# Widening the first inverses of a delta-rule kernel two steps at a time, with 64-row operands

## The chip, the cores and the metric

The kernel runs on one core of a Trainium2 chip. The metric is the device time of one execution in microseconds; the time before is a median of three runs.

## The reference

A linear attention with a delta rule (4 batches, 8 heads, 768 positions, head size 48) is followed by a gated MLP over the 384 joined channels. All is float32.

```python
k_n = k / (norm(k) + 1e-06)
for t in range(S):
    y[t]  = q[t] @ state
    v_old = k_n[t] @ state
    state = state + beta[t] * outer(k_n[t], v[t] - v_old)
x = y joined over heads                               # (4, 768, 384)
h = relu(x @ w_in); u, v = halves of h                # 1024 -> 512 + 512
v_n = (v - mean(v)) / sqrt(var(v) + 1e-06)
v_s = w_spatial @ v_n + b_spatial[:, None]            # over the 768 positions
out = (u * v_s) @ w_out
```

## The kernel before

**Tiling.** The positions are cut into chunks of 64, 12 per batch pair; two batch pairs give 24 steps (`NP`), each with 16 batch-head pairs laid out as 8 blocks (`NS`) on 128 partitions (two halves of 64). Within a chunk the recurrence is solved with the inverse of a unit triangular 64x64 matrix per batch and head. These inverses don't depend on the state, so they are made ahead of the steps, for groups of four steps (`GP`), six groups in all.

**Inverses.** `prep(g)` multiplies the keys with themselves on TensorE (`kk`), copies the products to SBUF, transposes the 32x32 diagonal blocks on VectorE so that one block lies along a partition (L651), scales them (L672), and solves them lane by lane (`lanes`, or `lanes16` for group 0) on the engine that `LANES` names: VectorE for groups 0, 2, 4, 5, GpSimd for groups 1 and 3. A second transposition (L730) puts the result back. Group 0 (`G16 = 1`) is solved for 16x16 blocks only, to have it sooner. `widen16(s)` then joins two 16x16 inverses to one 32x32, and `widen(g)` joins two 32x32 to one 64x64 for each step of the group, in five stages (`stage(f, e)`), where stage k finishes step k-1 and begins step k.

**`widen16` before.** For one step: a VectorE transposition of the blocks into `tn6` (L796); a TensorE burst E of 32 calls (8 blocks, 4 strips of 32 rows), each a 32x16 stationary block `kd` against a 32x16 one (L798); ScalarE negates the result into `gi` (L812); a burst F of 32 calls with 16-row operands (L805); VectorE adds the result into the block (L814); two half copies (L427) and two clears (L819) move the odd blocks to their place. `kd` is a copy of 16-column blocks made once (L654). Each float32 call is two matmul instructions in the trace, so a burst is 64 of them. All instructions of TensorE carry L587, the line of `mm`; the operand names tell them apart, and `kd` and `tn6` are parts of the tile `bbc`.

**Steps.** `step(s)` has five TensorE bursts (`a_`, `qs`, `b_`, `c_`, `pu`), with copies on ScalarE (L901, L931) and updates on VectorE (L872, L914, L916) between them; `b_` is the first that uses the 64x64 inverse. Two steps give one column block `J` of x, on which `mlp(J)` runs the first product of the MLP; `norm_v` makes mean and variance: ScalarE sums (L974, L984), and small instructions on VectorE (L981, L986, `fin`) work on two columns. After steps 11 and 23 `gate(b)` runs the spatial product and the output.

**What sets the order.** Every operation is added to a plan with an engine (or several to choose from), a cost in us, its reads and writes, and a priority: a due time (`due(s) = 38 + 8 s`) plus a correction from the table `TUNE`, one number per kind of operation. `Plan.run` is a list scheduler that simulates the engines with these costs and emits the instructions in the order of their planned starts. So each engine's order is fixed when the kernel is built, and every engine works its queue in order. `adv` and `execute` model TensorE's clock and its supply of instructions; `warm` fills idle TensorE time with products of `fl` that nobody reads. DMAs are all issued on SP.

**Storage.** Early tiles lie in storage that later holds weights and others. `kd` and `tn6` lie where the bias is loaded later; the raw parts of w_out and w_sp are loaded through two halves of `g0` (the pool `st`).

Of the kernel before, what the change touches and what calls it, by code (L numbers as in the profile page):

```python
# [1214 lines left out]
```

## Time and profile before

| | before |
|---|---|
| median of 3 runs | 471.94 us (469.5 to 472.24) |
| profiled execution | 473.46 us, its span 471.8 us |
| mean granted TensorE clock | 0.928 |
| busy: TensorE, VectorE, ScalarE, GpSimd | 424.1, 286.7, 239.4, 162.6 us |
| DMA | 40.67 MB |

The span runs from the first to the last instruction; all times within the trace count from its start. PE is TensorE, PEld its weight loads, DVE VectorE, ACT ScalarE, POOL GpSimd, SP SyncE. A granted clock of 1.00 is 2.4 GHz, 0.50 is 1.2 GHz.

### The profile page before, as it was taken

Reading aid. Unit: us, or ns where it says so; the run is one execution under the profiler, and the core shown is the slowest. Engines: PE = TensorE matmul, PEld = TensorE weight load, DVE = VectorE, ACT = ScalarE, POOL = GpSimd, SP = SyncE. Lnnn points to the kernel's source line nnn. Section 1 sums busy time; section 2 is a strip of 40 time slices with the busy share of each in tenths; the row PEclk is TensorE's granted clock in tenths of the full one; section 3 lists DMA queues with packets and bytes.
Section 4 is the critical chain, followed back from the end, with each engine's and each line's share of the span. In section 5 each row is a group of like instructions: output and inputs, shape, how many; then the busy total and the mean of one; then the engine's idle time right before and its main releaser. Section 6 shows DMA issues by size and latency. Waiting matters only on the chain.

```text
span 471.8 us, 20342 instructions
## 1 busy us (share of the span) xinstructions
PE 424.1 (90%) x9080; PEld 378.3 (80%) x9080; DVE 286.7 (61%) x635; ACT 239.4 (51%) x519; POOL 162.6 (34%) x294
## 2 busy tenths in 40 slices
PE   5827767998878999898999999999999999999997
PEld 4625666786766778787789999988899999999996
DVE  3998999998899964543399975423235222452340
ACT  3978737587941646994321248355323861131122
POOL 3339699883786985012217220000000000000000
PEclk9787555799978999999999999999999999999999
DMA  7950322651433452334433300133000011000002
GB/s 275 370 150 2 83 60 73 190 154 41 115 85 95 139 157 64 107 106 137 138 95 118 92 18 20 42 94 97 8 11 0 2 63 40 1 35 33 35 18 84
DMA packets 24456, 40.67 MB, mean 86 GB/s; under 512 B 3792, under 2 KB 14160, under 8 KB 24368
## 3 DMA queue, kind: packets, MB, share of 16 engines
q1 hardware_dynamic: 24368, 39.37, 27.2%
q8 instruction: 71, 1.16, 1.1%
q14 instruction: 17, 0.14, 0.1%
HBM read 33.46 MB, written 4.72 MB: 81 GB/s over the span
## 4 chain that ended last, share of the span: by engine, by line
PE 61%; DVE 15%; ACT 12%; DMA 5%; issue 4%; POOL 3%; SPq 1%; ACTq 0%; POOLq 0%; DVEq 0%
PE ps L587 61%; DMA bn<-in_bun 3%; DVE ps L697 2%; DVE prod L692 2%; ACT gt L984 1%; ACT vr L998 1%; ACT xt L788 1%; ACT vf L1006 1%; ACT pi L784 1%; ACT xt L427 1%; DVE pt L846 1%; DMA wout_h<-in_k_t 1%; DMA xs<-xs 1%; DVE ut L503 1%; DVE wla L482 1%
## 5 line engine op out<-in xcount | busy, mean ns | idle before, releaser
L587 PE MATMUL ps<-wsp_h,vf 128*128 128x256 f32 x480 | 96.6, 284 | 0.0
L587 PEld LDWEIGHTS ps<-wsp_h,vf 128*128 128x128 f32 x480 | 77.8, 188 | 0.9
L484 POOL TENSOR_TENSOR bn<-bn,nn 128x384 f32<-128x384 f32 x24 | 22.1, 920 | 95.7 <-DMA bn<-in_bun 41.2
L1065 DVE TENSOR_TENSOR gt<-ps,bbc 128x512 f32<-128x512 f32 x24 | 16.6, 690 | 53.6 <-PE ps L587 53.5
L692 POOL TENSOR_TENSOR wsp_h<-wsp_h 128x31 f32<-128x31 f32 (+15 forms) x62 | 36.8, 594 | 8.2 <-DVE wsp_h L672 6.1
L587 PE MATMUL ps<-wlb,vf 128*128 128x256 f32 x140 | 39.4, 281 | 0.0
L697 POOL TENSOR_TENSOR wsp_h<-wsp_h 128x60 f32<-128x60 f32 (+15 forms) x60 | 36.5, 609 | 1.7
L587 PE MATMUL ps<-bn 64*64 64x64 f32 x832 | 21.0, 244 | 14.2 <-DVE pt L846 6.3
L587 PEld LDWEIGHTS ps<-bn 64*64 64x64 f32 x832 | 17.3, 153 | 18.9 <-DVE pt L846 7.3
L697 DVE TENSOR_TENSOR ps<-ps,prod 128x192 f32<-128x192 f32 (+13 forms) x90 | 29.5, 328 | 2.3
L692 DVE TENSOR_TENSOR prod<-ps,la 128x192 f32<-128x192 f32 (+13 forms) x90 | 28.7, 319 | 2.2
L1070 ACT CAST xt<-gt 128x512 fp32r<-128x512 f32 x12 | 7.4, 620 | 41.9 <-DVE gt L482 41.8
L587 PE MATMUL ps<-wla,vf 128*128 128x256 f32 x100 | 28.1, 281 | 0.0
L1086 ACT COPY ob<-ps 128x384 f32<-128x384 f32 x24 | 11.5, 480 | 30.6 <-PE ps L587 24.8
L587 PE MATMUL ps<-wout_h,g 128*128 128x384 f32 x96 | 26.4, 342 | 0.0
L587 PEld LDWEIGHTS ps<-wlb,vf 128*128 128x128 f32 x140 | 26.3, 188 | 0.0
L587 PE MATMUL ps<-wout_h,xt 128*128 128x384 f32 x96 | 25.6, 338 | 0.0
L587 PE MATMUL ps<-wsp_h,bn 128*128 128x256 f32 x96 | 23.3, 281 | 0.0
L1030 ACT ACTIVATE ut<-ps 128x256 f32<-128x256 f32 x48 | 15.6, 377 | 13.8 <-PE ps L587 13.7
L1070 ACT CAST g<-gt 128x512 fp32r<-128x512 f32 x12 | 7.4, 619 | 28.5 <-DVE gt L482 21.1
L901 ACT COPY w<-ps 128x384 f32<-128x384 f32 x24 | 11.5, 479 | 19.9 <-PE ps L587 19.7
L846 DVE TENSOR_TENSOR pt<-ps,fl 128x512 f32<-128x512 f32 x24 | 16.3, 680 | 6.7 <-PE ps L587 6.6
(255 smaller groups left out, 1190.2 us busy)
## 6 DMA issues: line engine op xcount, KB each, us to landing
bn<-in_bun SPq DMA_DIRECT2D x44, 224.0 KB, 3.1
bn<-in_bun SPq DMA_DIRECT2D x48, 192.0 KB, 3.2
out<-ob SPq DMA_DIRECT2D x24, 192.0 KB, 1.9
vf<-in_w_in SPq DMA_DIRECT2D x6, 512.0 KB, 8.3
ke<-in_k_t SPq DMA_DIRECT2D x12, 224.0 KB, 3.0
g<-in_w_sp SPq DMA_DIRECT2D x6, 384.0 KB, 3.5
g<-in_w_out SPq DMA_DIRECT2D x4, 384.0 KB, 5.7
xs<-xs SPq DMA_DIRECT2D x22, 48.0 KB, 2.7
```

The source lines that it names most:

```text
L427: (nc.scalar.copy if e == "ACT" else ENG[e].tensor_copy)(out=out_, in_=in_)
L482: nc.vector.scalar_tensor_tensor(out=out, in0=in0, scalar=1.0, in1=in1, op0=ALU.mult, op1=op)
L484: nc.gpsimd.tensor_tensor(out=out, in0=in0, in1=in1, op=op)
L587: nc.tensor.matmul(o, l, r, start=start, stop=stop)
L692: P.add(eng, cost(n * m), lambda: ENG[eng].tensor_tensor(out=dst if fst else pt, in0=w[:, :n, j : j + 1].broadcast_to([128, n, m]), in1=la ...
L697: P.add(eng, cost(n * m), lambda: ENG[eng].tensor_tensor(out=dst, in0=dst, in1=pt, op=ALU.add), rd=[pk], wr=[key], pr=p0 + 2)
L846: P.add("DVE", 0.69, lambda: nc.vector.tensor_tensor(out=pt.rearrange("p (d c t) -> p d c t", d=2, t=64), in0=pq.rearrange("p (d c) -> p d ...
L901: P.add("ACT", 0.48, lambda: nc.scalar.copy(out=v3(w, 192), in_=v3(pc, 512)[:, :, 0:192]), rd=["pc"], wr=[("w", s % 2)], pr=pr)
L1030: nc.scalar.activation(out=dst[:, :, o * 128 : o * 128 + 128], in_=src[:, :, j], func=AF.Relu)
L1065: P.add("DVE", 0.69, lambda: nc.vector.tensor_tensor(out=gt(), in0=v3(bank(h.unit), 256), in1=bbc[0][:, th * 256 : th * 256 + 256].unsquee ...
L1070: P.add("ACT", 0.6, lambda: nc.scalar.copy(out=gv(gg)[0][:, hs], in_=gt_[t.unit]), rd=[kk], wr=[("gh", b, th, half)], pr=q)
L1086: P.add("ACT", 0.48, lambda: nc.scalar.copy(out=ob_[t.unit], in_=bank(h.unit)[:, :DM]), rd=[("po", b, th, o)], wr=[("ob", b, th, o)], pr=d ...
```

## The change

- `widen16(s)` works on two steps: it is called for s = 0 and 2. Both bursts use 64-row operands, 16 blocks by 2 halves, 32 calls each.
- The 64-row operands hold zeros outside their blocks. For E this is `e16` (2048 columns, cleared at the start, in the storage of group 4's inverses), for F `f16_()` (1024 columns in `g0`). They are filled by `masked`: a copy over all 128 partitions with a scale per partition, 1 in every second strip of 32 partitions and 0 in the others (`cst[:, 5:7]`), on ScalarE or GpSimd, two copies per operand.
- `kd` goes. The two halves of `g0` enter the pool `st` only after the last F.
- The clears after `widen` of the later groups may also go to ScalarE.
- In `norm_v` L981 and L986 go from VectorE to ScalarE.
- Some planner costs change, and all of `TUNE`; with it the order of every engine.

```diff
-    cst = new("cst", 4)
+    cst = new("cst", 7)
-    kd, tn6 = aux[:, 0:512], aux[:, 512:768]
+    tn6 = aux[:, 0:512]
+    e16 = tagged("xt1", GP * NS * 64)
+    def f16_():
+        return g0_()[:, 0:1024]
-    gi = early[4][:, 2048:2176]
+    gi = early[4][:, 2048:2304]
+    def masked(e, out_, in_, k):
+        if e == "ACT":
+            nc.scalar.activation(out=out_, in_=in_, func=AF.Copy, scale=cst[:, 5 + k : 6 + k])
+        else:
+            nc.gpsimd.tensor_scalar(out=out_, in0=in_, scalar1=cst[:, 5 + k : 6 + k], scalar2=None, op0=ALU.mult)
...
+    P.add("POOL", 0.5, lambda: nc.gpsimd.memset(e16, 0.0), wr=["E"], pr=-8)
-    P.pool("st", [0, 1])
+    P.pool("st", [])
...
         if g < G16:
-            P.add("ACT", 0.6, lambda: nc.scalar.copy(out=v3(kd, 16), in_=xg()[:, :, 0:16]), ...)
+            for k in range(2):
+                P.add("", {"ACT": 0.62, "POOL": 1.1}, lambda e, k=k: masked(e, v3(e16, 64)[:, :, k * 32 : k * 32 + 16], xg()[:, :, 0:16], k), ...)
...
     def widen16(s):
-        P.add("DVE", 0.44, lambda: nc.vector.transpose(out=v3(tn6, 32), in_=x8_()[:, :, 0:32]), rd=zd, wr=["tn6"], pr=pr)
+        P.add("DVE", 0.68, lambda: nc.vector.transpose(out=v3(tn6, 32), in_=x8_()[:, :, 0:32]), rd=zd, wr=["tn6"], pr=pr)
+        for k in range(2):
+            P.add("", {"ACT": 0.62, "POOL": 1.1}, lambda e, k=k: masked(e, v3(f16_(), 64)[:, :, k * 32 : k * 32 + 32], v3(tn6, 32), k), rd=["tn6", "cst"], wr=[F[k]], pr=pr)
         def e():
-            for q in range(NS):
-                for k in range(4):
-                    r = slice(32 * k, 32 * k + 32)
-                    mm(bank(u.unit)[32 * k : 32 * k + 16, q * 16 : q * 16 + 16], kd[r, (b0 + q) * 16 : (b0 + q) * 16 + 16], x8[r, q, 16:32])
+            for q in range(2 * NS):
+                for a in range(2):
+                    r = slice(64 * a, 64 * a + 64)
+                    mm(bank(u.unit)[r, q * 16 : q * 16 + 16], e16[r, (b0 + q) * 64 : (b0 + q) * 64 + 64], x8[r, q, 16:32])
         def f():
-            for q in range(NS):
-                for k in range(4):
-                    h = slice(32 * k, 32 * k + 16)
-                    mm(bank(u.unit)[32 * k : 32 * k + 32, 256 + q * 16 : 256 + q * 16 + 16], tn6[h, q * 32 : q * 32 + 32], gi[h, q * 16 : q * 16 + 16])
+            for q in range(2 * NS):
+                for a in range(2):
+                    r = slice(64 * a, 64 * a + 64)
+                    mm(bank(u.unit)[r, 256 + q * 16 : 256 + q * 16 + 16], f16_()[r, q * 64 : q * 64 + 64], gi[r, q * 16 : q * 16 + 16])
-        P.add("PE", 0.55, e, mode=3, ...)
+        P.add("PE", 1.86, e, mode=1, ...)
-        P.add("PE", 0.6, f, mode=4, ...)
+        P.add("PE", 1.86, f, mode=1, ...)
+        if s == G16 * GP - 2:
+            P.add("X", 0.0, None, wr=F, give=[("st", i) for i in range(2)])
...
     def norm_v(J, i0, i1):
-        P.add("DVE", 0.19, lambda: nc.vector.tensor_scalar_mul(out=f(1), in0=f(0), scalar1=-1.0 / DH), ...)
+        P.add("ACT", 0.2, lambda: nc.scalar.mul(out=f(1), in_=f(0), mul=-1.0 / DH), ...)
-        P.add("DVE", 0.19, lambda: nc.vector.tensor_scalar(out=f(3), in0=f(2), scalar1=1.0 / DH, scalar2=EPS, op0=ALU.mult, op1=ALU.add), ...)
+        P.add("ACT", 0.2, lambda: nc.scalar.activation(out=f(3), in_=f(2), func=AF.Identity, scale=1.0 / DH, bias=cst[:, 3:4]), ...)
...
-            for k in range(GP if g < G16 else 0):
+            for k in range(0, GP if g < G16 else 0, 2):
                 widen16(s + k)
```

Left out of the diff: the new table `TUNE`; the planner's costs of a DMA's landing (1.2 to 1.6), of the MLP's chunks (0.232, 0.117, 0.175 per matmul to 0.236, 0.119, 0.178), of a clear of 1056 columns (1.0 to 0.5) and of GpSimd's half copies (1.05 to 0.9).

## Rows read from the trace of the kernel before

**Rows 1.** The page's first part: busy us, share of the span, instructions.
```profile
PE 424.1 (90%) x9080; PEld 378.3 (80%) x9080; DVE 286.7 (61%) x635; ACT 239.4 (51%) x519; POOL 162.6 (34%) x294
```

**Rows 2.** Windows by stage: length, busy us (x instructions), granted clock, DMA share, GB/s.
```profile
43.90:77.92 34.02, 22.13 (x1097) 19.60 (x1089) 30.46 (x73) 21.25 (x45) 28.38 (x52) 0.57 0.24 64
...
83.60:118.30 34.70, 33.43 (x944) 26.44 (x945) 30.52 (x65) 24.77 (x53) 24.37 (x44) 0.92 0.44 126
118.30:163.20 44.90, 38.12 (x1237) 31.74 (x1237) 41.01 (x105) 23.80 (x61) 36.57 (x76) 0.89 0.38 109
163.20:244.40 81.20, 75.17 (x2232) 63.43 (x2232) 43.58 (x90) 49.93 (x114) 26.83 (x40) 1.00 0.40 115
244.40:471.80 227.40, 223.39 (x2932) 212.30 (x2932) 99.42 (x214) 84.11 (x187) 19.73 (x41) 1.00 0.14 44
```

**Rows 3.** The chain that ended last: start us, us, what.
```profile
45.05 1.79 issue
...
83.58 10.94 PE ps L587 x298
```

**Rows 4.** Timeline: start us, us, engine, line, operation, operands, shape, count.
```profile
40.14 2.25 DVE L730 STREAM_TRANSPOSE wla<-wl 128x1024 f32<-128x1024 f32 x1
...
47.04 0.69 PE L587 MATMUL ps<-ke 64*64 64x64 f32 x32
...
52.21 1.13 PE L587 MATMUL ps<-ke 64*64 64x64 f32 x32
...
78.80 1.05 PE L587 MATMUL ps<-bn,wla 64*64 64x48 f32 x32
```

**Rows 5.** Waits of TensorE in 40 to 92: us in total, times, longest.
```profile
PE ps L587 <- issue: 8.0, 6, 1.8
```

**Rows 6.** Windows of the instructions on tile bbc alone (kd and tn6).
```profile
43.90:47.04 3.14, 1.34 (x128) 1.22 (x128) 0.00 (x0) 0.00 (x0) 0.00 (x0) 1.00 0.02 5
...
51.23:53.27 2.04, 1.05 (x64) 0.94 (x64) 0.45 (x1) 0.00 (x0) 0.00 (x0) 0.50 0.42 107
...
43.90:77.92 34.02, 7.17 (x512) 6.24 (x512) 3.20 (x6) 2.73 (x5) 0.00 (x0) 0.57 0.24 64
```

**Rows 7.** Groups of instructions by line, 0 to 100: busy us, mean ns, idle before.
```profile
L427 ACT COPY wla<-wla 32x256 f32<-32x256 f32 x7 | 2.8, 403 | 5.9 <-DVE wla L814 5.8
L819 POOL MEMSET wla<- 32x256 f32 x8 | 2.7, 341 | 3.6 <-DVE tn L779 2.8 <-POOL wsp_h L692 0.5
...
L427 ACT COPY wsp_h<-wsp_h 32x1024 f32<-32x1024 f32 x2 | 2.1, 1042 | 0.0
...
L796 DVE STREAM_TRANSPOSE bbc<-wla 128x256 f32<-128x256 f32 x4 | 1.7, 420 | 0.6 <-PE ps L587 0.6
...
L812 ACT ACTIVATE wlb<-ps 128x128 f32<-128x128 f32 x4 | 1.1, 276 | 2.6 <-PE ps L587 2.4
...
L814 DVE TENSOR_TENSOR wla<-wla,ps 128x128 f32<-128x128 f32 x4 | 1.0, 257 | 0.0
```

**Rows 8.** Timeline of ScalarE and GpSimd at several places.
```profile
11.99 0.62 ACT L654 COPY bbc<-wla 128x512 f32<-128x512 f32 x1
...
42.19 1.26 POOL L484 TENSOR_TENSOR win_l<-ut,win_h 128x512 fp32r<-128x512 f32 x1
...
44.30 0.98 POOL L456 MEMSET wl<- 128x1056 f32 x1
...
100.39 0.28 POOL L697 TENSOR_TENSOR wsp_h<-wsp_h 128x31 f32<-128x31 f32 x1
...
107.14 0.95 POOL L742 MEMSET wlb<- 32x1024 f32 x1 [0.54 <-DVE tn L779]
...
118.31 0.48 ACT L901 COPY w<-ps 128x384 f32<-128x384 f32 x1 [0.35 <-PE ps L587]
```

**Rows 9.** Windows of the instructions of L981, then of L986: VectorE's busy us.
```profile
118.30:163.20 44.90, 1.89 (x3) 0.89 0.38 109
...
118.30:163.20 44.90, 0.83 (x3) 0.89 0.38 109
```

More of the change, by code (lines that the diff above doesn't have):

```diff
@@ L287, in run @@
                 dma = max(dma, t + 1.0) + o.kb / 300.0
-                o.end = dma + 1.2 + o.lag
+                o.end = dma + 1.6 + o.lag
             for p, h in o.rel:
@@ L427, in copy, with clear @@
         (nc.scalar.copy if e == "ACT" else ENG[e].tensor_copy)(out=out_, in_=in_)
+    def masked(e, out_, in_, k):
[3 more added lines that the diff above has]
+            nc.gpsimd.tensor_scalar(out=out_, in0=in_, scalar1=cst[:, 5 + k : 6 + k], scalar2=None, op0=ALU.mult)
+    def clear(e, g, a):
+        r = slice(a * 64 + 32, a * 64 + 64)
+        out_ = xt_of(g)[r, 0:2048].rearrange("p (b c) -> p b c", c=64)[:, :, 0:32]
+        if e == "ACT":
+            nc.scalar.copy(out=out_, in_=cst[r, 4:5].unsqueeze(2).broadcast_to([32, 32, 32]))
+        else:
+            ENG[e].memset(out_, 0.0)
     P.pool("pq", [0])
@@ L622, in prep @@
             sl = slot(s)
[L623 removed]
+            P.add("PE", 0.51, kk, mode=1, tail=0.185, act=0.427, rd=[kk_], wr=bk + [("kk", s)] + [("x", sl, z) for z in ("d0", "o0", "z1", "d1")] + ([("E", k) for k in range(2)] if g == 4 else []), pr=pk + s4)
             o = xslot(s)
@@ L732, in prep @@
             rd=[W], wr=xp("d0") + xp("z1"), pr=p0 + 3)
-        if any(x[0] == q for x in LANES[g + 1 :]):
+        nxt = [i for i in range(g + 1, NG) if LANES[i][0] == q]
+        if nxt and nxt[0] >= G16:
             if g < G16 or lane == "POOL":
@@ L752, in go @@
             return bbc[0]
-        ld(go, b_sp.unsqueeze(0).broadcast_to([128, SEQ]), wr=["kd", "tn6", "bbc"] + [(("wout", i), "e") for i in range(ND)], pr=due(12), kb=384)
+        ld(go, b_sp.unsqueeze(0).broadcast_to([128, SEQ]), wr=["tn6", "bbc"] + [(("wout", i), "e") for i in range(ND)], pr=due(12), kb=384)
     def widen(g):
@@ L780, in widen @@
                 rd += ["tn", ("x", slot(s), "o0")]
-            P.add("PE", 0.53, lambda f=f, e=e: stage(f, e), mode=2, tail=0.165, act=0.213 * n, inst=32 * n, rd=rd, wr=[("pe", g)], pr=pr, acq=[("pm", u)] if k == 0 else [])
+            P.add("PE", 0.53, lambda f=f, e=e: stage(f, e), mode=2, tail=0.165, act=0.213 * n, inst=32 * n, rd=rd + ([("pe", g - 1)] if g and not k else []), wr=[("pe", g)], pr=pr, acq=[("pm", u)] if k == 0 else [])
             last = k == GP
@@ L791, in widen16 @@
     def widen16(s):
-        o, sl, b0 = xslot(s), slot(s), s % GP * NS
-        x8_ = lambda: v3(xt_of(s // GP)[:, o : o + 512], 64)
+        o, b0 = xslot(s), s % GP * NS
+        x8_ = lambda: v3(xt_of(s // GP)[:, o : o + 1024], 64)
         pr = due(s) - 9
-        zd, u = [("x", sl, "d0"), ("x", sl, "z1")], Hold()
-        P.add("DVE", 0.44, lambda: nc.vector.transpose(out=v3(tn6, 32), in_=x8_()[:, :, 0:32]), rd=zd, wr=["tn6"], pr=pr)
+        xz = lambda z: [("x", slot(s + t), z) for t in range(2)]
@@ L822, in load @@
+            P.add("", {"DVE": 0.45, "POOL": 0.75}, port=True, bias=BIAS, fn=lambda e, r=r: ENG[e].memset(x8_()[r, :, 0:32], 0.0), rd=[("zb", s, a)], wr=[("zc", s, a)], pr=pr)
+        P.add("X", 0.0, None, rd=[(z, s, a) for z in ("zb", "zc") for a in range(2)], wr=xz("z1") + xz("d1"))
     def load(s):
@@ L980, in norm_v @@
         k, q, ii = ("sj", J), due(2 * J + 1) + 14, (i0, i1)
-        P.add("DVE", 0.19, lambda: nc.vector.tensor_scalar_mul(out=f(1), in0=f(0), scalar1=-1.0 / DH), rd=[("st", i) for i in ii], wr=[k], pr=q, port=True)
+        P.add("ACT", 0.2, lambda: nc.scalar.mul(out=f(1), in_=f(0), mul=-1.0 / DH), rd=[("st", i) for i in ii], wr=[k], pr=q)
         for j, i in enumerate(ii):
@@ L1024, in mlp_u @@
         first = o == 0 and half == 0
-        chunks(mms, 3, 0.117, [("xh", J), ("xl", J), "win"] + ([] if first else [("ua", b0, th)]), [("pu", J, half)] + ([("ua", b0, th)] if first else []), pr, [("pm", h)] + ([("u", u_h[b0 + j, th]) for j in range(2)] if o == 0 and half == 0 else []), [(xp_(J), x)])
+        chunks(mms, 3, 0.119, [("xh", J), ("xl", J), "win"] + ([] if first else [("ua", b0, th)]), [("pu", J, half)] + ([("ua", b0, th)] if first else []), pr, [("pm", h)] + ([("u", u_h[b0 + j, th]) for j in range(2)] if o == 0 and half == 0 else []), [(xp_(J), x)])
         def ev(j):
@@ L1058, in mlp_g @@
         wr = [("pg", b, th, half)] + ([] if half else [("ga", b, th)]) + ([("gdone", b)] if (th, half) == (NT // 2 - 1, 1) else [])
-        chunks(mms, 3, 0.117, rd, wr, pr, [("pm", h), ("gt", t)] + ([("g", gg)] if half == 0 else []), [("full", full_h[b * NT + i]) for i in range(NT)])
+        chunks(mms, 3, 0.119, rd, wr, pr, [("pm", h), ("gt", t)] + ([("g", gg)] if half == 0 else []), [("full", full_h[b * NT + i]) for i in range(NT)])
         gt = lambda: v3(gt_[t.unit], 256)
```

45 lines of the change are left out of this document (24 added, 21 removed), and 49 rows, old and new, of the table TUNE.

## The prediction

> **What bounds the kernel now.** I read the busy shares first: TensorE is busy 90% of the span, the other engines far less [rows 1]. A share over the whole span mixes stages, so the windows by stage come next [rows 2]. From 244.40 on TensorE is busy 223.39 of 227.40 us, and from 83.60 to 118.30 33.43 of 34.70: there it is a full queue, and only removed TensorE work or a filled gap pays. Before 83.60 it is otherwise. Between 43.90 and 77.92 TensorE is busy 22.13 of 34.02 us, at a mean granted clock of 0.57, while VectorE is busy 30.46 and GpSimd 28.38. The chain that ended last says when the full queue begins: the first long unbroken TensorE piece starts at 83.58 [rows 3]. So an early delay counts whole, since all later TensorE work queues behind it, and an early gain counts as long as there is work to put into it.
>
> What fills the early stretch? The inverses of group 0 come out of the transposition that ends at 40.14 + 2.25 = 42.39, and the first multiplication of step 1 that uses a widened inverse starts at 78.80 [rows 4]: 36.4 us, of which the change rewrites a part. TensorE issues 1097 matmuls in 34.02 us, 31 ns each [rows 2]. It has six pauses of 8.0 us in total in 40 to 92 that wait for nothing the profile shows ("issue") [rows 5], the longest on the chain at 45.05, in the middle of the first widening burst [rows 3]. I read this as a limit on how fast instructions come, not on how fast they run: a packed group of 32 matmuls of 64x64 takes 0.69 us at full clock (22 ns each) and 1.13 us (35 ns each) at half [rows 4].
>
> **The change part by part.** *TensorE instructions.* The widening 16 to 32 is 512 of the 1097 matmuls, 7.17 us busy [rows 6]. The new form does two steps in a burst of 64 for E and 64 for F, so 4 bursts and 256 matmuls. Removed: 256 x 31 ns = 7.9 us of issue.
>
> *Length of a burst.* No row shows a 64-row block used on the diagonal alone. The nearest is the packed group of 32, which uses four quadrants at once; the new burst uses two. Lower bound, if a matmul costs what it does there: 64 x 22 = 1.4 us at full clock, 64 x 35 = 2.3 at half (1.2 of 2.4 GHz). Upper bound, if half the quadrants means half the speed: 2.8 and 4.5. The moving side has 16 columns instead of 64, so I take the middle, 2.1 and 3.4. Their issue share is 64 x 31 ns = 2.0. The first old burst ran at clock 1.00, a later one at 0.50 [rows 6]; taking one new burst at full and three at half clock, the excess over issue is 0.1 + 3 x 1.4 = 4.3 us. Issue minus excess: a gain of 3.6 us. Bounds: all four at the low value gain 7.9 - 4 x 0.3 = 6.7; all four at the high one lose 4 x 2.5 - 7.9 = 2.1. A rule speaks against the change here: the Trainium skill (TensorE: Matmul & The Clock Gate, "Packing small matmuls — row/col tiling") has matmuls on different 32-row strips run side by side, which the zero-padded 64-row operand gives up. The same page ("LDWEIGHTS (loading the stationary operand)") prices a weight load by its columns alone, columns / 1.2 in ns; 32 loads of 64 columns in a row on each half would be 1.7 us by it, an estimate, and with that at any clock the gain would be the whole 7.9. No run here shows such a burst yet.
>
> *The other engines in the widening.* Removed [rows 7]: four transpositions of 0.42, four additions of 0.26, four negations of 0.28, eight half copies of 0.40, eight clears of 0.34, and one 0.62 copy of the 16-column blocks [rows 8]: 10.3 us over three engines. Added: two transpositions of twice the width (0.42 to 0.84 each, say 0.7), two additions of 0.45, two negations of 0.4, four copies of 32x512 (between 0.40 for 256 and 1.04 for 1024 columns [rows 7], so 0.6), four clears of 0.5 (between 0.34 and 0.95 for the same widths [rows 7, 8]), and six scaled copies of 128x512. For these ScalarE's 128x512 copy at 11.99 is the nearest, 0.62; on GpSimd a 128x512 two-operand instruction takes 1.26 and a 1056-column clear 0.98, so 0.5 to 1.3 [rows 8]. With 0.65 each the sum is 1.4 + 0.9 + 0.8 + 2.4 + 2.0 + 3.9 = 11.4. That is no saving; it is the same work in two rounds instead of four. I count it at zero on the path, covered by the E burst that runs while the scaled copies are made; without the cover two scaled copies, 1.3 us, stand before each F burst, 2.6 in all. The new clear of the 2048-column operand at the start (about 2 x 0.98 on GpSimd) and six small constants lie before GpSimd's first need; cover gone, 2 us.
>
> *Waits added.* E's operand shares storage with the inverses of group 4, and w_out's and w_sp's loads on SP now wait until the last F burst has read its operand; SP's queue behind that wait holds nothing that steps 0 to 3 need if the plan places it so. Neither weight is used before the first gate. Zero; cover gone, a load of step 2 or 3 starts later by as much as the last F burst is late.
>
> *Statistics moved to ScalarE.* L981 and L986 leave VectorE, 1.89 + 0.83 = 2.7 us of its time in 118.30 to 163.20 [rows 9]. There VectorE is busy 41.01 of 44.90, TensorE idles 6.8, and ScalarE has room (23.80) [rows 2]. Bounds 0 and 2.7; I take 1.5, a little over half: TensorE does wait there, but not behind every instruction of VectorE.
>
> *Order.* All priorities are new and the planner's TensorE and DMA costs rise a little, so every queue is another. No row prices it. Its scale is TensorE's idle time between 83.60 and 244.40, 1.3 + 6.8 + 6.0 = 14 us [rows 2]: a third of it, 4.7, either way goes into the range, zero into the sum.
>
> **Sum.** -3.6 - 1.5 = -5.1 us. The profiled execution took 473.46 (span 471.8), so 468.4; it lies 1.5 above the median of 471.94, so 466.8 for the median.
>
> **Rivals.** *No change, held at step 4.* Steps 4 to 7 need group 1's inverses, made on GpSimd alone, whose last lane ends at 100.67; step 4's first copy starts at 118.31 [rows 8]. Until then TensorE lives on what steps 0 to 3 set free, with 1.3 us idle in 34.7. If steps 0 to 3 come 3.6 earlier and group 1 doesn't, that work is spent 3.6 earlier and the gain returns as idle time: 471.94 - 1.5 = 470.4. It decides if GpSimd takes scaled copies: six at 1.26 are 7.6 us against 3.1 us of clears and copies that leave it. Against it: GpSimd is idle 10 us in 83.60 to 118.30 [rows 2], so a new order has room.
>
> *Slower, bursts bound by running.* Place: 43.9 to 78, at half clock. If the pauses are not owed to the number of instructions, the 256 fewer give nothing, and widening goes from 7.17 us busy to 4 x 3.4 = 13.6 with F directly on the way to step 0: +6.4, less 1.5, 476.8. It decides when a burst takes more than 2.0 + 7.9 / 4 = 4.0 us or when the pauses stay. For it: a half clock in the whole stretch. Against it: 31 ns a matmul over 34 us, between the 22 and the 35 that the groups need, and pauses inside a burst whose operands were all there. The Trainium skill (Runtime: NRT & Kernel Launch, "Instruction fetch mechanics") holds that fetching is hidden behind issue, and by that rule the pauses would stay, this rival; the 1.79 us pause at 45.05 does not look like it.
>
> *A better order than the sum says.* The early gain at its upper bound 6.7, 2.7 from the statistics and 4.7 of filled idle: 471.94 - 14.1 = 457.8. It belongs to the forecast's own side.
>
> **How the numbers follow.** The forecast, a gain of over 1% (about what a measurement of this kernel can tell from no change), has 0.47, its upper end 457.8 included; held at step 4 or otherwise within 1% has 0.29; slower has 0.24, by the long bursts (0.14) or by a worse order (0.10). The likeliest is 466.8, its own range 458 to 467. The range of 8 in 10 leaves out a tenth on each side: 458 to 476.
>
> **What would show it.** Right: 128 + 128 matmuls for the widening and under 3.6 us a burst; pauses for "issue" in 40 to 92 well under 8.0 us; step 1's first use of a widened inverse near 75 instead of 78.80; the full queue beginning 3 to 5 us before 83.58; TensorE's idle time in 83.6 to 118.3 still near 1.3. Wrong: a full queue that begins earlier and an idle stretch before step 4 (held); bursts over 4 us (slower); a begin that is unchanged and a time that moved all the same (order alone).

## The result, and the profile after

The changed kernel takes 467.55 us (median; 465.84 to 470.79). The kernel before, timed beside it, takes 472.2. The ratio is 0.9906, 95% interval 0.9887 to 0.9925: faster by 4.4 us by that ratio, 0.94%. The profiled execution took 466.53 us, its span 464.8, at a mean granted clock of 0.949 (0.928 before). The prediction said 466.8. The median lies just above the forecast's own range of 458 to 467 and inside 458 to 476; by the cut at 1% it falls, by a hair, to the side "within 1%", which had a chance of 0.29 against 0.47 for the forecast.

The total came out close. Where the time went is another matter, and most of this part is about that. First the page's first part, as in [rows 1]: busy us, share of the span, instructions.

```profile
PE 420.9 (91%) x8824; PEld 375.4 (81%) x8824; DVE 281.2 (61%) x615; ACT 247.7 (53%) x542; POOL 163.9 (35%) x289
```

TensorE has 256 instructions fewer, as counted beforehand. ScalarE gained 8.3 us of work, VectorE lost 5.5. Next the windows of [rows 2], the last one to the new end: length, busy us (x instructions) of the five engines, granted clock, DMA share, GB/s.

```profile
43.90:77.92 34.02, 29.29 (x996) 26.38 (x988) 30.86 (x64) 28.78 (x54) 31.60 (x44) 0.74 0.35 100
83.60:118.30 34.70, 31.43 (x975) 25.14 (x967) 28.75 (x69) 23.47 (x56) 23.74 (x49) 0.95 0.43 124
118.30:163.20 44.90, 41.18 (x1326) 33.82 (x1328) 40.82 (x101) 27.51 (x68) 38.57 (x73) 1.00 0.37 107
163.20:244.40 81.20, 76.20 (x1888) 66.89 (x1877) 40.67 (x83) 49.26 (x112) 17.12 (x30) 1.00 0.32 96
244.40:464.80 220.40, 215.60 (x3118) 202.07 (x3116) 101.03 (x212) 88.91 (x202) 22.36 (x41) 1.00 0.16 50
```

The first window holds about 100 matmuls fewer and 7 us more busy time, and its clock is 0.74 instead of 0.57. In 83.60 to 118.30 TensorE idles 3.27 us, before 1.27. In 118.30 to 163.20 the granted clock is 1.00 instead of 0.89, and TensorE is busy 3.1 us more. From 244.40 on it is a full queue, as before. Now the widening itself, on the timeline of VectorE and TensorE (`wla,xt` is E, `wlb,g` is F; a few records of each burst stand apart).

```profile
46.02 2.02 DVE L756 STREAM_TRANSPOSE wla<-wl 128x1024 f32<-128x1024 f32 x1
...
48.60 1.94 PE L611 MATMUL ps<-wla,xt 64*64 64x16 f32 x62
...
50.93 1.99 PE L611 MATMUL ps<-wla,xt 64*64 64x16 f32 x64
...
54.32 3.49 PE L611 MATMUL ps<-wlb,g 64*64 64x16 f32 x62
...
61.53 3.44 PE L611 MATMUL ps<-wlb,g 64*64 64x16 f32 x62
```

The windows of the second and the third burst, columns as above, give the clock:

```profile
50.93:52.92 1.99, 1.99 (x74) 1.90 (x66) 1.33 (x1) 1.94 (x4) 1.91 (x4) 1.00 0.36 90
54.32:57.81 3.49, 3.49 (x72) 3.49 (x74) 3.49 (x7) 3.42 (x6) 3.25 (x4) 0.50 0.27 70
```

Two bursts run at full clock in 2.0 us, two at half clock in about 3.5. And the waits of TensorE in 40 to 92, as in [rows 5]: us in total, times, longest.

```profile
PE ps L611 <- issue: 2.7, 2, 1.4
```

So the pauses fell from 8.0 to 2.7 us. But L756, group 0's second transposition, now starts at 46.02 instead of 40.14 [rows 4]: group 0 is solved 5.65 us later (it ends at 48.04 instead of 42.39). Most of it is there before the lanes begin: the first lane starts at 22.40 instead of 17.27, because VectorE now waits 2.21 us for ScalarE up to 15.35 and takes group 1's first transposition (19.27) ahead of group 0's scaling. With that steps 0 and 1 come later than before (first copy of `w` at 69.22 and 81.47, before 65.55 and 79.92), in spite of the shorter way. The gain appears at step 4, as the timeline of GpSimd, VectorE and ScalarE shows; compare [rows 8].

```profile
96.53 0.83 POOL L508 TENSOR_TENSOR bn<-bn,nn 128x384 f32<-128x384 f32 x1 [1.24 <-PE ps L611]
97.32 0.39 POOL L723 TENSOR_TENSOR wsp_h<-wsp_h 128x31 f32<-128x31 f32 x1
...
98.49 2.33 DVE L756 STREAM_TRANSPOSE wlb<-wsp_h 128x1024 f32<-128x1024 f32 x1
...
101.64 1.97 DVE L675 STREAM_TRANSPOSE wsp_h<-xt 128x1024 f32<-128x1024 f32 x1
...
112.55 0.48 ACT L934 COPY w<-ps 128x384 f32<-128x384 f32 x1
```

Group 1's last lane ends at 97.71 (before 100.67) and step 4 copies its first `w` at 112.55 (before 118.31): 5.8 us earlier, 3.0 of them before the last lane ends and 2.8 after. The chain that ended last, as in [rows 3], has the TensorE piece that answers to the one at 83.58 now at 82.00; from 211.10 on two TensorE pieces make up most of it.

```profile
82.00 6.60 PE ps L611 x194
...
211.10 81.66 PE ps L611 x1698
304.86 156.49 PE ps L611 x1783
```

### The profile page after: what moved, and what is told of

Its sections match the earlier page's. It is cut to its first block, busy times and chain, and to the rows that moved or that the text cites. A ratio compares the mean times of both kernels' runs of the same rounds, so it can differ in the third digit from the quotient of the medians.

```text
span 464.8 us, 19799 instructions
## 1 busy us (share of the span) xinstructions
PE 420.9 (91%) x8824; PEld 375.4 (81%) x8824; DVE 281.2 (61%) x615; ACT 247.7 (53%) x542; POOL 163.9 (35%) x289
## 4 chain that ended last, share of the span: by engine, by line
PE 69%; ACT 12%; DVE 10%; issue 4%; DMA 2%; POOL 2%; SPq 1%; ACTq 0%; POOLq 0%; DVEq 0%
PE ps L611 69%; DMA xs<-xs 1%; DVE xt L756 1%; DMA wout_h<-in_k_t 1%; ACT gt L1017 1%; ACT vr L1007 1%; SPq L465 1%; DVE ut L527 1%; DVE pt L879 1%; ACT xt L433 1%; ACT wsp_h L433 1%; ACT xt L445 1%; POOL wlb L433 1%; ACT xs L964 1%; DVE tn L806 1%
## 5 line engine op out<-in xcount | busy, mean ns | idle before, releaser
L611 PE MATMUL ps<-wsp_h,vf 128*128 128x256 f32 x480 | 92.4, 283 | 0.0
L611 PEld LDWEIGHTS ps<-wsp_h,vf 128*128 128x128 f32 x480 | 76.2, 188 | 0.5
L718 POOL TENSOR_TENSOR wsp_h<-wsp_h 128x31 f32<-128x31 f32 (+15 forms) x62 | 39.3, 635 | 18.1 <-DVE wsp_h L698 8.8
L611 PE MATMUL ps<-wlb,vf 128*128 128x256 f32 x144 | 40.4, 281 | 0.0
L723 POOL TENSOR_TENSOR wsp_h<-wsp_h 128x60 f32<-128x60 f32 (+15 forms) x60 | 37.7, 629 | 2.2
L611 PE MATMUL ps<-bn 64*64 64x64 f32 x832 | 19.9, 238 | 15.4 <-DVE pt L879 8.9
L611 PE MATMUL ps<-wla,vf 128*128 128x256 f32 x96 | 27.0, 281 | 0.0
L611 PE MATMUL ps<-wsp_h,bn 128*128 128x256 f32 x96 | 21.3, 281 | 0.0
L1007 ACT ACTIVATE vr<-ps 128x512 f32<-128x512 f32 x22 | 13.2, 598 | 13.4 <-PE ps L611 13.3
L1031 ACT ACTIVATE vr<-vr,st 128x512 f32<-128x512 f32 x22 | 17.1, 813 | 5.6 <-DVE st L1027 5.6
```

The source lines that it names most:

```text
L611: nc.tensor.matmul(o, l, r, start=start, stop=stop)
L718: P.add(eng, cost(n * m), lambda: ENG[eng].tensor_tensor(out=dst if fst else pt, in0=w[:, :n, j : j + 1].broadcast_to([128, n, m]), in1=la ...
L723: P.add(eng, cost(n * m), lambda: ENG[eng].tensor_tensor(out=dst, in0=dst, in1=pt, op=ALU.add), rd=[pk], wr=[key], pr=p0 + 2)
L1007: P.add("ACT", 0.6, lambda: nc.scalar.activation(out=raw_(r), in_=bank(h.unit), func=AF.Relu, accum_out=st[:, j : j + 1]), rd=[("pv", i)], ...
L1031: P.add("ACT", 0.81, lambda j=j, i=i: nc.scalar.activation(out=raw_(raw_h[i]), in_=raw_(raw_h[i]), func=AF.Identity, scale=g(6, j), bias=g ...
```

## The experiments

**The question.** The change has three parts: 64-row bursts, statistics on ScalarE, a new order. My theory was the sum of the prediction: bursts -3.6, statistics -1.5, order 0. The rivals: the order did it all; the gain is held at step 4. In all kernels below the plan is left as it was, so each engine issues the same operations in the same order, except where the edit says otherwise. Step dates are the starts of the copies of `w`; each comes from one profiled execution, and such dates move by 1 to 2 us from one execution to another where nothing was changed (step 0 comes at 69.22 in the kernel after and at 68.04 in `a_norm_dve`). The profiled execution of the kernel before lay 1.3 us above the median beside it and that of the kernel after 1.0 below its own, so late dates make the gain look larger than the medians do. The mean granted clock doesn't order the kernels: it was 0.946 in `a_rows32` and 0.945 in `a_both`, which gained nothing, against 0.928 before. Ratios are to the kernel before, timed beside each.

| kernel | group 1's last lane ends | step 1 | step 4 | step 8 | step 23 | ratio, 95% interval |
|---|---|---|---|---|---|---|
| before | 100.67 | 79.92 | 118.31 | 155.27 | 341.91 | 1 |
| b_norm_act | 100.37 | 79.95 | 117.89 | 155.11 | 340.64 | 1.0029, 1.0004 to 1.0054 |
| b_rows64 | 101.92 | 80.85 | 120.75 | 157.81 | 341.43 | 1.0042, 1.0019 to 1.0065 |
| b_rows64_nomask | 100.77 | 80.03 | 118.53 | 154.41 | 339.95 | 1.0018, 0.9997 to 1.0039 |
| b_lane_short | 100.56 | 79.82 | 118.33 | 154.60 | 342.26 | 1.0015, 0.9990 to 1.0040 |
| b_dvefree | 100.17 | 77.47 | 117.91 | 154.11 | 341.77 | 0.9973, 0.9944 to 1.0002 |
| b_dvefree_rows64 | 98.78 | 75.43 | 116.56 | 152.33 | 338.54 | 0.9966, 0.9937 to 0.9995 |
| after | 97.71 | 81.47 | 112.55 | 152.04 | 336.48 | 0.9906, 0.9887 to 0.9925 |
| a_norm_dve | 96.98 | 80.28 | 111.95 | 153.85 | 338.48 | 0.9959, 0.9931 to 0.9987 |
| a_rows32 | 100.93 | 84.55 | 115.57 | 156.41 | 342.12 | 1.0000, 0.9975 to 1.0026 |
| a_both | 100.83 | 84.23 | 115.69 | 157.14 | 343.77 | 1.0079, 1.0053 to 1.0104 |
| a_lane_long | 97.58 | 78.94 | 112.98 | 155.66 | 341.44 | 0.9978, 0.9949 to 1.0007 |
| a_gate1 | 94.54 | 80.19 | 114.85 | 154.43 | 339.14 | 0.9979, 0.9953 to 1.0006 |
| a_gate2 | 94.86 | 80.08 | 117.30 | 159.05 | 344.13 | 0.9990, 0.9963 to 1.0017 |

### The bursts, in the new order

`a_rows32` is the kernel after with the old 32-row bursts, now of 128 matmuls for two steps, and the scaled copies kept.

```diff
-                for a in range(2):
-                    r = slice(64 * a, 64 * a + 64)
-                    mm(bank(u.unit)[r, q * 16 : q * 16 + 16], e16[r, (b0 + q) * 64 : (b0 + q) * 64 + 64], x8[r, q, 16:32])
+                for k in range(4):
+                    r, c = slice(32 * k, 32 * k + 32), (b0 + q) * 64 + k % 2 * 32
+                    mm(bank(u.unit)[32 * k : 32 * k + 16, q * 16 : q * 16 + 16], e16[r, c : c + 16], x8[r, q, 16:32])
...
```

> The changed kernel with its own order, but each of the four bursts made of 128 matmuls on 32-row strips instead of 64 on 64-row halves; scaled copies stay. Theory 1: the 128 more matmuls per pair of bursts bring the pauses for issue back (2.7 us in 40 to 92 becomes about 7), step 1's first use of its inverse moves 3 to 4 us later and the ratio to the kernel before goes to about 0.998. Theory 2: the early stage moves by up to 4 us but the end by less than 1, ratio 0.990 to 0.993.

The whole gain goes: ratio 1.0000. The rows show it in the bursts. First TensorE's timeline of `a_rows32`.

```profile
47.72 1.28 PE L611 MATMUL ps<-wla,xt 32*16 32x16 f32 x128
...
49.56 0.27 PE L611 MATMUL ps<-wla,xt 32*16 32x16 f32 x15
...
51.75 1.11 PE L611 MATMUL ps<-wla,xt 32*16 32x16 f32 x113 [1.92 <-issue]
...
55.31 0.80 PE L611 MATMUL ps<-ke 64*64 64x64 f32 x18 [1.83 <-issue]
```

Its waits in 40 to 92:

```profile
PE ps L611 <- issue: 8.8, 7, 1.9
```

And the window from the end of group 0's transposition to step 0, of `a_rows32` and then of the kernel after:

```profile
47.06:72.69 25.63, 17.38 (x872) 15.60 (x876) 19.88 (x42) 17.09 (x31) 20.83 (x27) 0.60 0.33 98
```

```profile
48.04:69.22 21.18, 20.08 (x622) 19.29 (x626) 18.80 (x40) 17.07 (x32) 19.41 (x23) 0.62 0.37 107
```

The first burst of 128 runs in 1.28 us, 10 ns a matmul. The next stops after 15 and waits 1.92 us with all its operands there. Such pauses also fall inside bursts of the 64x64 form (`ke`, 1.83 us), which speaks for the number of instructions as their cause and not for the 32-row form; no run changes the one without the other. Over the stretch the 64-row form has 2.70 us more running and 7.15 us less idle (25.63 - 17.38 = 8.25 against 1.10), 4.45 us net. At the end the two kernels differ by 0.0094 x 472 = 4.4 us (1.5 either way). So, within that, the early gain is kept to the end here, and the balance of issue against running is shown by rows of one stretch.

The Trainium skill (Runtime: NRT & Kernel Launch, "Instruction fetch mechanics") holds that fetching hides behind issue. This trace doesn't look like a supply that is always hidden: the pauses come back with the 256 instructions (8.8) and go with them (2.7). Whether fetching is what is late, or another part of the supply, no run here shows.

### The statistics, in both orders

`a_norm_dve` puts L1014 and L1019, the two small instructions, back on VectorE; `b_norm_act` moves them to ScalarE in the kernel before.

```diff
-        P.add("ACT", 0.2, lambda: nc.scalar.mul(out=f(1), in_=f(0), mul=-1.0 / DH), ...)
+        P.add("ACT", 0.2, lambda: nc.vector.tensor_scalar_mul(out=f(1), in0=f(0), scalar1=-1.0 / DH), ...)
...
-        P.add("ACT", 0.2, lambda: nc.scalar.activation(out=f(3), in_=f(2), func=AF.Identity, scale=1.0 / DH, bias=cst[:, 3:4]), ...)
+        P.add("ACT", 0.2, lambda: nc.vector.tensor_scalar(out=f(3), in0=f(2), scalar1=1.0 / DH, scalar2=EPS, op0=ALU.mult, op1=ALU.add), ...)
```

> The changed kernel with its own order of instructions, only the two small statistics operations put back on VectorE at the same places. Theory 1, the terms of my sum (3.6 us from the 64-row bursts, 1.5 us from the statistics): 1.5 us slower than the changed kernel, ratio to the kernel before about 0.994. Theory 2, the new order brings the gain and the edits bring little: within 0.5 us of the changed kernel, ratio 0.990 to 0.992.

> The kernel before with its own order, only the two small statistics operations moved to ScalarE at the same places. Theory 1: 1.5 us faster, ratio 0.997. Theory 2: ratio 0.999 to 1.001.

In the new order the move is worth 0.0053 x 472 = 2.5 us (1.6 either way). In the old order it is worth nothing, if anything 1.4 us the other way: 1.0029, with TensorE's wait for the state update (`s` L914) in 112 to 164 at 1.5 us before and 1.7 in `b_norm_act`. At step 7 `a_norm_dve` and the kernel after agree (143.55 and 143.64); at step 8 it is 1.8 behind. VectorE in `a_norm_dve`, and TensorE's wait for the state update in 112 to 164:

```profile
145.16 1.61 DVE L1014 TENSOR_SCALAR st<-st 128x2 f32<-128x2 f32 x1 [0.44 <-ACT vr L1007]
148.71 0.60 DVE L1019 TENSOR_SCALAR st<-st 128x2 f32<-128x2 f32 x1
150.66 0.43 DVE L1027 SCALAR_TENSOR_TENSOR st<-st 128x2 f32<-128x2 f32 x1
```

```profile
PE ps L611 <- DVE s L947: 2.2, 1, 2.2
```

The kernel after, ScalarE and VectorE at the same place, and the same wait:

```profile
145.24 0.20 ACT L1014 ACTIVATE st<-st 128x2 f32<-128x2 f32 x1
147.37 0.30 ACT L1019 ACTIVATE st<-st,cst 128x2 f32<-128x2 f32 x1
...
148.81 0.40 DVE L1027 SCALAR_TENSOR_TENSOR st<-st 128x2 f32<-128x2 f32 x1
```

```profile
PE ps L611 <- DVE s L947: 0.6, 1, 0.6
```

The instruction on two columns takes 1.61 us on VectorE, where the same line took 0.37 at 123.00 (`a_both` has 1.60 at this place, so it is no chance), and stands in the queue ahead of the state update L947, for which TensorE waits. Off that queue, TensorE's wait falls from 2.2 to 0.6 us, 1.6 of the 1.8 by which step 8 moves.

### Both undone: what the order is worth

`a_both` is the kernel after with both edits, each as above:

```diff
+                    mm(bank(u.unit)[32 * k : 32 * k + 16, q * 16 : q * 16 + 16], e16[r, c : c + 16], x8[r, q, 16:32])
...
+        P.add("ACT", 0.2, lambda: nc.vector.tensor_scalar_mul(out=f(1), in0=f(0), scalar1=-1.0 / DH), ...)
...
```

> The changed kernel's order with both edits undone: 32-row bursts and statistics on VectorE. Singly they cost 4.5 and 2.5 us. Theory A, the new order pays only together with the edits it was made for, and the two sit in different stretches: the losses add, 7 us, ratio 1.004 to 1.007, slower than the kernel before. Theory B, the order alone has a value and the losses overlap: ratio 0.998 to 1.001.

Ratio 1.0079: without the two edits the new order is 3.7 us slower than the kernel before (1.2 either way). It still has the widening in pairs of steps and the scaled copies that the 64-row operands need, so the 3.7 us are the price of the order with these; no run has the order by itself. Within it the bursts are worth 0.0120 x 472 = 5.7 us when the statistics stay on VectorE and 4.4 when they don't; the statistics 3.7 with 32-row bursts and 2.5 with 64-row ones (each 1.5 to 1.8 either way). Loss and gains are +3.7, and -8.2 together.

### The bursts, in the old order

`b_rows64` gives the kernel before 64-row bursts, one step at a time, with the scaled copies on ScalarE. `b_rows64_nomask` leaves F's copies out, and one of E's two.

```diff
-                for k in range(4):
-                    r = slice(32 * k, 32 * k + 32)
-                    mm(bank(u.unit)[32 * k : 32 * k + 16, q * 16 : q * 16 + 16], kd[r, (b0 + q) * 16 : (b0 + q) * 16 + 16], x8[r, q, 16:32])
+                for a in range(2):
+                    r = slice(64 * a, 64 * a + 64)
+                    mm(bank(u.unit)[r, q * 16 : q * 16 + 16], e16[r, (b0 + q) * 64 : (b0 + q) * 64 + 64], x8[r, q, 16:32])
...
+        P.add("DVE", 0.44, lambda: [nc.vector.transpose(...)] + [masked(v3(gt_[s % 2], 64)[:, :, k * 32 : k * 32 + 32], v3(tn6, 32), k) for k in range(2)], ...)
```

> The kernel before with its own order, one step at a time as before, but with 64-row operands: 32 matmuls a burst instead of 64, 256 fewer in all, the operands filled by scaled copies on ScalarE. Theory 1: the pauses for issue in 40 to 92 fall from 8.0 to about 3 us and the full queue begins 3 us earlier, ratio about 0.993. Theory 2: the pauses fall, the early stage moves up to 3 us earlier, but the end moves by less than 1 us because group 1's inverses on GpSimd hold step 4 at 118, ratio 0.998 to 1.001.

> The kernel before, its order kept, with 64-row bursts of 32 matmuls per step, and the scaled copies for F left out and those for E reduced to one, so that ScalarE has the same instructions as in the kernel before; the inverses are wrong by that. The same bursts with the scaled copies were 2 us slower than the kernel before. Theory E, the scaled copies on ScalarE ate the bursts' gain: step 1's first copy moves from 79.92 to 77 or earlier and the ratio is 0.992 to 0.995. Theory F, in the old order the pauses of TensorE were covered by waits for other engines: ratio 0.998 to 1.001.

Both take the pauses away; of `b_rows64_nomask` the waits in 40 to 92 and step 1's copy:

```profile
PE ps L597 <- issue: 0.4, 1, 0.4
```

```profile
80.03 0.48 ACT L911 COPY w<-ps 128x384 f32<-128x384 f32 x1
```

7.6 of the 8.0 us of pauses are gone, and step 1 is where it was (79.92). So in the old order the pauses were covered. With the copies (`b_rows64`) steps 1 and 4 come 0.9 and 2.4 later, and the ratio is 1.0042. My zero for the copies needed a cover that this order doesn't give; the two ratios overlap, so their price is not settled beyond "not a gain".

What covered the pauses? VectorE works without a gap from 61.3 to 82 in both kernels, on group 2's lanes, w_out's conversion and the pieces of the widening in one queue. Two rows show it: the window of the kernel before, columns as above, and ScalarE's wait for VectorE in 42 to 82 of `b_rows64_nomask` (5.8 us before).

```profile
61.30:82.00 20.70, 15.18 (x624) 13.82 (x622) 19.80 (x53) 9.96 (x23) 19.38 (x40) 0.50 0.26 69
```

```profile
ACT wla L428 <- DVE wla L824: 6.5, 3, 4.4
```

In that stretch VectorE's last two additions of the widening (L814, here L824) start at 64.84 and 72.58 before and at 64.95 and 72.69 with the shorter bursts. In the new order VectorE has room: in `a_rows32` it idles 5.75 of the 25.63 us above. `b_dvefree` leaves 28 of group 2's lane instructions out; `b_dvefree_rows64` does so on top of `b_rows64_nomask`.

```diff
                 lanes("DVE", 0, 16, wq, "wp", prod, PR, lambda x: 0.157 + 1.04e-3 * x, j)
+                if g == 2 and 4 <= j <= 17:
+                    P.ops[-1].fn = P.ops[-2].fn = lambda: None
```

> The kernel before, its order kept, with 28 of the lane instructions of group 2 on VectorE left out (j = 4 to 17, both instructions each; in the kernel before they lie between 63.2 and 80.4 us and take some 10.6 us; group 2's inverses are then not solved). The widening keeps its 32-row bursts of 64 matmuls a step. Theory F, VectorE's queue sets the dates of steps 0 and 1 in this order: step 1's first w copy (79.92 before) comes 4 us or more earlier. Rival, TensorE's issue pauses set them: step 1 moves by less than 1.5 us. Then, of the time: if step 4 is held by group 1's inverses, whose second transposition can't start before the last lane on GpSimd ends (100.7), step 4 stays within 1.5 us of 118.31 and the time within 0.4% of the kernel before; if early gains count whole, the time falls by as much as step 1 comes earlier, some 1%.

> As b_dvefree, the same lane instructions of group 2 left out, and the widening with 64-row bursts of 32 matmuls for one step (F's scaled copies left out, one scaled copy for E). Theory F: with VectorE's queue cleared TensorE's bursts are what is left, so step 1 comes a further 2 to 4 us earlier than in b_dvefree, where without the clearing the same bursts moved it by nothing; pauses for issue under 1 us instead of some 8. Rival, the bursts are covered whatever VectorE does (by ScalarE's copies or the steps' loads): step 1 within 1 us of b_dvefree. Time: within 0.4% of b_dvefree if step 4 is held by group 1's inverses, 0.4 to 0.8% under it if not.

Steps 1 and 4 of `b_dvefree`, then of `b_dvefree_rows64`:

```profile
77.47 0.48 ACT L903 COPY w<-ps 128x384 f32<-128x384 f32 x1 [0.91 <-PE ps L587]
...
117.91 0.48 ACT L903 COPY w<-ps 128x384 f32<-128x384 f32 x1 [0.35 <-PE ps L587]
```

```profile
75.43 0.48 ACT L913 COPY w<-ps 128x384 f32<-128x384 f32 x1
...
116.56 0.48 ACT L913 COPY w<-ps 128x384 f32<-128x384 f32 x1 [0.35 <-PE ps L597]
```

With VectorE's queue cleared step 1 comes 2.45 us earlier, less than the 4 expected, and the same 64-row bursts that moved it by nothing now move it by a further 2.0. Both are clear of chance: the other kernels of this order without F's scaled copies have step 1 at 79.82 to 80.03. That fits the theory that VectorE's queue covered the pauses, with TensorE close behind it. The times hardly follow: of the 2.45 us, 0.4 are left at step 4 and 0.1 at step 23; of the 4.5 us of `b_dvefree_rows64`, 1.75 at step 4. By the ratios the two gain 1.3 and 1.6 us (1.4 either way). This is what the rival "held at step 4" says.

### What holds step 4

In the old order the distance from the end of group 1's last lane to step 4 is 17.5 to 17.8 us in six of the seven kernels (18.8 in `b_rows64`), in the new order 14.6 to 15.4 in all where nothing was moved. So step 4 goes with the last lane, at a distance that the order sets; these dates alone don't tell whether it follows the lane or both follow TensorE. A part of the 3.0 us by which the last lane moved is order too: in the kernel before a piece of w_out's conversion (`g`) stands between the last lanes on GpSimd (98.29, 1.03 us after a wait of 0.50), in the kernel after the pieces come behind them (98.26 and 99.27). Two differences of order are seen in the distance: VectorE now takes group 1's second transposition (98.49) ahead of group 3's first one (101.64), where before it stood behind it (99.78 and 101.77); and group 2's second transposition, at 112.63 before, now comes after step 4, at 124.46. I take these for the 2.8 us; no run separates them.

What sets the last lane? Two kernels tried it: `b_lane_short` leaves six lane instructions of group 1 out, `a_lane_long` adds seven clears among them.

```diff
                 lanes("POOL", 0, 32, w3, W, prod, PR, lambda x: 0.21 + 1.75e-3 * x, j)
+                if g == 1 and j in (8, 9, 10):                                   # b_lane_short
+                    P.ops[-1].fn = P.ops[-2].fn = lambda: None
...
+                if g == 1 and j == 22:                                           # a_lane_long
+                    P.ops[-2].fn = lambda f0=P.ops[-2].fn: [nc.gpsimd.memset(gt_[1], 0.0) for _ in range(7)] + [f0()]
```

> The kernel before, its order kept, with six of group 1's lane instructions on GpSimd left out (about 0.6 us each, 3.6 us together), so that group 1's inverses are incomplete. Theory C: the second transposition of group 1 moves from 101.77 to about 98, step 4 from 118.31 to about 115 and the ratio to about 0.993. Theory D: ratio 0.998 to 1.000.

> The changed kernel with seven clears of 512 columns (about 0.48 us each, 3.4 us together) added on GpSimd in the middle of group 1's lanes. Theory C, group 1's inverses decide when step 4 starts and all later work hangs on step 4: step 4's first copy moves from 112.55 to about 116 and the ratio to the kernel before goes from 0.991 to about 0.997. Theory D, TensorE's queue is full by then and hides it: under 1 us, ratio 0.990 to 0.993.

`b_lane_short` moved nothing: the last lane ends at 100.56. The instructions left out would have run between 47 and 55, and there GpSimd now waits longer:

```profile
50.24 0.84 POOL L821 MEMSET wla<- 32x256 f32 x2 [3.23 <-DVE tn L781]
53.57 0.30 POOL L821 MEMSET wla<- 32x256 f32 x1 [2.49 <-ACT wla L427]
```

GpSimd works in order, and between group 1's lanes stand the half copies and clears of group 0's widening. In the kernel before the first clear waited 1.78 us and the third 0.50; by 61.2 the two kernels are level (61.20 and 61.26). So the run took away nothing that set a date, and does not test the lanes as such. What it shows is how the bursts reach step 4: a later widening holds the lanes queued behind its clears and copies. `a_rows32` has the same thing as a loss; in the kernel after this copy starts at 59.20 without a wait.

```profile
60.70 0.61 POOL L433 COPY wla<-wla 32x512 f32<-32x512 f32 x1 [2.88 <-DVE hd L687]
```

In `a_rows32` the last lane ends 3.2 us later than in the kernel after, about the 3.0 that separates their steps 4. Further on other work stands between the lanes: a scaling of `bn`, an operand of a step, that waits for TensorE, and a part of w_out's conversion that waits for VectorE. The waits of GpSimd in 90 to 101 of `b_lane_short`:

```profile
POOL g L484 <- DVE g L482: 1.1, 1, 1.1
POOL bn L484 <- PE ps L587: 1.0, 1, 1.0
```

`a_lane_long` was 3.4 us slower than the kernel after (0.9978 against 0.9906). Its steps 0 to 3 came 2 to 3 us earlier than in the kernel after, its last lane and step 4 at the same time, and GpSimd went into the last lane without a wait, where the kernel after waits 1.24 us for TensorE (96.53). That supports the lanes as what step 4 follows. But the time was lost later: step 4 is 0.4 us behind the kernel after, step 7 3.0. Windows of `a_lane_long`:

```profile
108.00:114.00 6.00, 4.21 (x96) 3.30 (x96) 4.11 (x13) 4.67 (x12) 0.51 (x2) 0.72 0.27 74
...
138.00:144.00 6.00, 4.40 (x144) 3.49 (x146) 4.67 (x15) 1.93 (x7) 6.00 (x12) 0.76 0.14 38
```

TensorE idled there, and its granted clock fell from 1.00 to half for part of each, which the kernel after avoids from 90 to 163. How much of the 3.4 us is the clock is not separated.

Last, two attempts at a faster kernel. `a_gate1` takes the kernel after and moves the last lane's addition ahead of the `bn` scaling, and the transposition ahead of the five VectorE instructions between it and the state update; `a_gate2` also moves the end of w_out's conversion behind group 1's copies. `behind(i, ...)` puts the operations that it lists right behind operation i in the finished order.

```diff
+    behind(161, 162, 163, 702, 1216, 1209)      # last lane's addition, L756, then L905, L587, L506
+    behind(168, 1219, 1220)                     # a_gate2 alone, and two more like it
```

> The kernel after, with five instructions moved in the queues and nothing else: the last addition of group 1's lanes goes ahead of a scaling of bn on GpSimd that waits for TensorE (96.53), and group 1's second transposition (98.49 after) goes ahead of four VectorE instructions, behind the state update at 95.17. Theory, step 4 is held by group 1's inverses: the transposition starts near 96, but GpSimd's next copy (100.95 after) stands behind two 128x384 instructions of w_out's conversion (98.26 and 99.27), so only ScalarE's copy (101.84 after) and the first stage of the widening come 2 us earlier; step 4 comes 0 to 1.5 us before 112.55, and the time is within 0.4% of the kernel after, 0.987 to 0.993 of the kernel before. Rival, steps and MLP work set it: step 3's delayed update (VectorE's L905) and w_out's parts make TensorE wait, step 4 stays or comes later, and the time rises by up to 1 us.

> As a_gate1, and the four instructions that end w_out's conversion (two on GpSimd, one each on ScalarE and VectorE) moved behind group 1's last copy and clear, so that nothing stands between the transposition and the widening of group 1. Theory, step 4 is held by group 1's inverses: the copy on GpSimd starts near 98.5 instead of 100.95, step 4 comes 2 to 2.5 us before 112.55, and the time falls by up to as much, to 0.985 to 0.990 of the kernel before. Rival, the gain returns as idle time of TensorE further on (the full queue begins at 211 in the kernel after, and steps 5 to 7 are held by group 2's inverses or by statistics): step 4 earlier, time within 0.2% of the kernel after.

Both are slower than the kernel after. VectorE in `a_gate1`:

```profile
94.57 2.29 DVE L756 STREAM_TRANSPOSE wlb<-wsp_h 128x1024 f32<-128x1024 f32 x1
...
98.73 0.56 DVE L506 SCALAR_TENSOR_TENSOR wout_l<-g,wout_h 128x384 fp32r<-128x384 f32 x1 [0.99 <-DMA g<-in_w_sp]
...
101.78 0.43 DVE L806 STREAM_TRANSPOSE tn<-wlb 128x256 f32<-128x256 f32 x1
```

The transposition comes 3.9 us earlier, yet the first use of its result, L806, comes 0.5 later than in the kernel after (101.28), and step 4 2.3 later. The edit was a poor one: it put L506 behind w_sp's load into the half of `g` that L506 reads, so VectorE waited 0.99 us for that load, and one of the four pieces of w_out's low part is made from what the load left there. What the runs do show is that the transposition's own date is not enough: L806 stands behind products of the next steps for which VectorE waits on TensorE. Whether a clean reordering gains was not tried.

## Why the prediction came out right

**Instructions and burst length: right.** 256 fewer; 2.0 us at full clock and 3.5 at half against 2.1 and 3.4. My middle between the bounds held (64 records at half clock would be 3.6), and the argument for it (16 moving columns, not 64) is as good as the two numbers. One assumption was off: two bursts ran at full clock, not one. The price of weight loads alone that the Trainium skill has (TensorE: Matmul & The Clock Gate, "LDWEIGHTS (loading the stationary operand)") gave an estimate of 1.7 at any clock; the trace has 1.94 to 1.99 at full and 3.44 to 3.49 at half, so the clock counts.

**Issue: right.** The pauses fell from 8.0 to 2.7 us with the instructions and came back with them. The rival "bursts bound by running" falls with that.

**Early gain, -3.6: right mechanism, and the size within the noise.** Between the end of group 0's transposition and step 0 the new form saves 4.45 us, and 4.4 to 5.7 at the end (1.5 to 1.8 either way). The terms were 7.9 of issue and 4.3 of excess; the rows have 7.15 and 2.70. The excess was mis-sized most: two bursts at full clock cost next to nothing over issue. But it is true of the new order only. In the old order the pauses were covered by VectorE's queue and the same bursts gain nothing, which the prediction did not see: it read 8 us of TensorE pauses as 8 us on the path, while VectorE was busy 30.46 of the same 34.02 us [rows 2].

**Other engines, 0: not settled.** The wider instructions cost about as estimated: the transposition 0.70, the addition 0.42, the negation 0.37, a scaled copy on ScalarE 0.72. The two scaled copies that GpSimd took ran 1.57 each, above the 1.3 that I allowed, so the six are 6.0 us and not 3.9. In the old order the copies made steps later; in the new one no run prices them.

**Statistics, -1.5: likely too small.** 2.5 to 3.7 us in the new order (1.6 and 1.7 either way), nothing in the old. The upper bound of 2.7 was the busy time that leaves VectorE, and that was the wrong measure. What counts is what stands behind the instruction in the queue: one that waits there or is stretched delays the state update, and TensorE with it.

**Order, 0: wrong.** Without the two edits the new order, with its scaled copies, costs 3.7 us, inside the 4.7 that I allowed either way. The total came out because this error and two gains that were larger than forecast nearly cancel, and that is luck: the prediction's -5.1 is +3.7 - 8.2 = -4.5 in the runs, if the order is counted first. Counted the other way round, each edit in the old order brings nothing (1.0029 and 1.0042), and the whole gain appears only with the order. So neither "the order did it all" nor my sum describes it: the gain belongs to the edits and the order together.

**Where the gain would show: wrong.** I looked for step 1 earlier and a full queue beginning 3 to 5 us before 83.58. Step 1 came 1.5 us later, the long piece of the chain began at 82.00, and TensorE's idle time in 83.60 to 118.30, which should have stayed near 1.3, is 3.3. The new order spends the shorter widening on a later group 0 and takes the gain at step 4.

**The rival "held at step 4": the old order bears it out.** In `b_dvefree` an early gain of 2.45 us is down to 0.4 at step 4. In the new order group 1's lanes moved too, and the gain stayed. The prediction looked at GpSimd's free time; what ties the lanes to group 0 and its steps is the instructions queued between them, which wait for the widening and for TensorE.

## What to carry to other kernels

A pause on the busiest engine is worth its length only if no other in-order queue runs beside it without a gap; look for that queue before pricing the pause, and price an edit together with the order it will run in, since here each edit alone gained nothing in the old order. An instruction moved off a crowded queue is worth the wait of what stands behind it, not its own busy time. And an early gain survives only if the next group's work, on whatever engine, moves with it: read what is queued between its instructions.
